# Where the partial sums of the second layer's first product lie in PSUM

## The chip, the core and the metric

The kernel runs on one core of a Trainium2 chip. The metric is the device time of one execution in microseconds (us). The engines are TensorE (PE, with its weight loads as PEld), VectorE (DVE), ScalarE (ACT), GpSimd (POOL) and SyncE (SP), whose queue issues the DMA transfers. Each engine works through its own list of instructions in order, and waits at an instruction until what it needs has been signalled. PSUM, where TensorE leaves its sums, has eight banks here, each of 128 x 512 fp32 values.

## The reference

Attention over chunks of 32 tokens with a local window and 8 memory keys, then two feed-forward layers one behind the other on its 3072 x 512 result:

```python
x = attention(q, k, v, mem_k, mem_v)        # 4 x 8 heads x 768 tokens x 64
h = x @ moe_w_in                            # 3072 x 512 by 512 x 2048
x = (h * sigmoid(1.702 * h)) @ moe_w_out    # 2048 x 512
h = x @ moe2_w_in
return (maximum(h, 0) + alpha * minimum(h, 0)) @ moe2_w_out
```

Weights come as 64-bit floats; the kernel rebuilds fp32 from their words, and splits each fp32 operand into a high and a low fp32r part. A product of two operands is then three matmuls: high by high, high by low, low by high.

## The kernel before

The program has three stages. First come attention and, woven into it, the first layer, in six blocks of 512 tokens: `mm1` (line 425), `act1`, `split_g` and `mm2_t` (line 481), with the second layer's weights prepared beside it. `finish1` (lines 486 to 493) takes the four accumulators of a block, in the PSUM pairs `ya` and `yb`, to `o` tiles by DVE (halves 0 and 2) and ACT (1 and 3), and stores them.

The second layer runs in three rounds (`for P in range(NPAIR)`, line 859) of 1024 tokens each. Its products are done by Strassen's scheme: seven products of half-size blocks in place of eight, in the Winograd form, named p1 to p7 and worked in the order p1, p5, p6, p3, p7, p2, p4 (`PRODUCTS`, line 495). A round has two parts:

- `first` (lines 606 to 644), called for eight blocks (`fp` 0 to 7): for each of the seven products six matmuls of 128x128 by 128x512 (line 619), 42 in a block. Products p1, p6, p7 and p4 add up in one chain, x; p5 and p3 in another, y; p2 stands alone in z. In between the chains are read: behind p1, p5 and p6 ACT copies the state of the chain to SBUF (`snap`, line 603: s1, s5, u2), and behind p3, p7 and p2 DVE adds a copy to it (line 636); p4 is read by the two activation steps of `act2_ops` (lines 452 and 454). So x is read between p1 and p6, between p6 and p7, and between p7 and p4; y between p5 and p3.
- `second` (lines 699 to 751): seven products of 48 matmuls (line 717), four steps of 12 each, from operands that ACT and DVE make just ahead (the ring, lines 657 to 675), with both halves m = 0 and 1 of a tile in use.

PSUM tiles come from pools. `pair(tag, name)` (line 270) gives a tile of two banks; the tags `a`, `ya` and `yb` have one place each, that is six banks, and the tag `h` has two places of one bank each. A new tile of a tag waits until the last readers of the place are done; inside a tile the framework orders a write behind the reads of that tile that stand before it in the program. `two_banks` (line 589) hands out `a`, `ya`, `yb` in rotation: one pair for each block of `first`, whose halves are x and y, and one pair each for x, y and z in `second`.

All instructions of the second layer carry `kp` (line 439), which keeps them in the written order on each engine. `background` (line 458) puts waiting DVE and ACT work (the rest of the activation, the ring) behind the products by a written clock that counts 0.2275 us for a matmul; it is not moved by what really happens. Weight tiles of the second layer stream through ten places, issued by SP ten ahead of their use (`s_ahead`, lines 567 to 585); a block of `first` uses three tiles of 512 KB and one of 256 KB. The last step of the first layer, `do_mm2(len(steps) - 1)`, is called from inside the first block of the layer, behind p5 (lines 643 and 864).

Of the kernel before, what the change touches and what calls it, by code (L numbers as in the profile page):

```python
# [9 lines left out]
F32 = mybir.dt.float32  # L10
# [25 lines left out]
TBM = 512  # L36
# [22 lines left out]
def fused_kernel(ctx: ExitStack, tc: tile.TileContext, qs, ks, vs, ident, w_in1, w_out1, w_in2, w_out2, alpha, out):  # L59
# [10 lines left out]
    ps2 = ctx.enter_context(tc.tile_pool(name="ps2", bufs=2, space=PSUM))  # L70
# [199 lines left out]
    def pair(tag, name):  # L270
        return ps1.tile([128, 2, DM], F32, tag=tag, name=name)
# [147 lines left out]
    def mm1(p, x, n, f):  # L419
        h = ps2.tile([128, TBM], F32, tag="h", name=f"h{p}")  # L420
        wh, wl = wt[p, f]
        i = 0
        for k in range(NKC):
            for w, z in ((wh, 0), (wh, 1), (wl, 0)):
                nc.tensor.matmul(  # L425
                    h[:, :n], w[:, 0, k * 128:(k + 1) * 128], x[:, z, k, :n], start=(i == 0), stop=(i == 3 * NKC - 1)
                )
                i += 1
        return h
# [15 lines left out]
    def vec(cost, fn, after=0.0):  # L445
        clock["v"] = max(clock["v"], after) + cost
        fn()

    def act2_ops(out, c, f, cost):
        t = gp.tile([128, TBM], F32, tag="t", name="t")  # L450
        return [
            (cost, lambda: kp(nc.vector.tensor_scalar(
                out=t, in0=c, scalar1=0.0, scalar2=al_sb[:, f:f + 1], op0=ALU.min, op1=ALU.mult))),
            (0.67, lambda: kp(nc.vector.scalar_tensor_tensor(
                out=out, in0=c, scalar=0.0, in1=t, op0=ALU.max, op1=ALU.add))),
        ]

    def background(until, slot):

        while True:  # L460
            q = later if later else rings if rings and rings[0][2] <= slot else fills if fills and fills[0][2] <= slot else None
            if q is None or clock["v"] + q[0][0] > until:
                return
            cost, fn = q.pop(0)[:2]
            vec(cost, fn)
# [117 lines left out]
    def s_done(n):  # L583
        streamed[1] += n
        s_ahead(streamed[1] + 10)

    npair = [0]

    def two_banks():
        t = pair(("a", "ya", "yb")[npair[0] % 3], f"acc{npair[0]}")  # L590
        npair[0] += 1
        return t

    graw = {}

# [5 lines left out]
    def snap(src, tag, name):  # L601
        t = gp.tile([128, TBM], F32, tag=tag, name=name, bufs=2)
        kp(nc.scalar.copy(t, src))  # L603
        return t

    def first(P, fp, after1=None):
        t = two_banks()
        acc = {"x": t[:, 0], "y": t[:, 1]}
        kept = {}
        for d, n in enumerate(PRODUCTS):  # L610
            if n == "p2":
                acc["z"] = ps2.tile([128, TBM], F32, tag="h", name="hz")
            to = acc[{"p1": "x", "p6": "x", "p7": "x", "p4": "x", "p5": "y", "p3": "y", "p2": "z"}[n]]
            w = units[P, "a", fp, d // 2][:, d % 2]
            hi, lo = xops[P][n]
            i = 0
            for k in range(2):
                for c, x in ((0, hi), (0, lo), (1, hi)):
                    kp(nc.tensor.matmul(  # L619
                        to, w[:, c, k * 128:(k + 1) * 128], x[:, k], start=(i == 0 and n not in ADDED), stop=(i == 5),  # L620
                        skip_group_check=n in ADDED,
                    ))
                    i += 1
            clock["pe"] += 6 * T_MM
            background(clock["pe"], NPROD * fp + d)
            if n == "p1":
                kept["s1"] = snap(to, "gh", "s1")
            elif n == "p5":
                kept["s5"] = snap(to, "gl", "s5")
            elif n == "p6":  # L630
                kept["u2"] = snap(to, "gh", "u2")
            else:
                with_, f, th = {"p3": ("u2", fp, 1), "p7": ("s5", fp + NFP, 1), "p2": ("s1", fp, 0), "p4": (None, fp + NFP, 0)}[n]
                out = graw[f // 2, th][:, f % 2]
                if with_ is not None:
                    vec(0.69, lambda: kp(nc.vector.tensor_tensor(out=out, in0=to, in1=kept[with_], op=ALU.add)), clock["pe"])  # L636
                    later.extend(act2_ops(out, out, f, 0.45))
                else:
                    for cost, fn in act2_ops(out, to, f, 0.75):
                        vec(cost, fn, clock["pe"])  # L640
            if d % 2 == 1 or d == 6:
                s_done(1)
            if n == "p5" and after1 is not None:
                after1()
# [54 lines left out]
    def second(P):  # L699
        acc = {}  # L700
        kept = {}
        last = P == NPAIR - 1
        for q, (d, jj) in enumerate(order):
            n = PRODUCTS[d]
            while (P, d, jj) not in made:
                cost, fn = (later or rings).pop(0)[:2]
                vec(cost, fn)
            key = {"p1": "x", "p6": "x", "p7": "x", "p4": "x", "p5": "y", "p3": "y", "p2": "z"}[n]
            if key not in acc:
                acc[key] = two_banks()  # L710
            to = acc[key]
            hi, lo = ring.pop((P, d, jj))
            w = units[P, "b", d, jj]
            tail = n == "p4" and jj == 3
            for ft, m in [(a, b) for b in range(2) for a in range(2)] if tail else [(a, b) for a in range(2) for b in range(2)]:
                for i, (c, g) in enumerate(((0, hi), (0, lo), (1, hi))):
                    kp(nc.tensor.matmul(  # L717
                        to[:, m], w[:, ft, c, m * 128:(m + 1) * 128], g[:, ft],
                        start=(jj == 0 and ft == 0 and i == 0 and n not in ADDED), stop=(jj == 3 and ft == 1 and i == 2),
                        skip_group_check=n in ADDED,  # L720
                    ))
            clock["pe"] += 12 * T_MM
            background(clock["pe"], NPROD * NFP + q)
            s_done(1)
            while stores:
                kp(nc.sync.dma_start(out=stores[0][0], in_=stores.pop(0)[1]))
            if jj < 3:
                continue
            if n in ("p1", "p5", "p6"):
                tag = {"p1": "gh", "p5": "gl", "p6": "t"}[n]  # L730
                kept[n] = [snap(to[:, m], tag, "k") for m in range(2)]
                continue
            with_, mh, th = {"p3": ("p6", 0, 1), "p7": ("p5", 1, 1), "p2": ("p1", 0, 0), "p4": (None, 1, 0)}[n]
            for m in range(2):
                o = op.tile([128, TBM], F32, tag="o", name="o2")
                r = 256 * mh + 128 * m
                cols = out[r:r + 128, P * PAIR + th * TBM:P * PAIR + (th + 1) * TBM]
                if with_ is not None:
                    vec(0.69, lambda: kp(nc.vector.tensor_tensor(out=o, in0=to[:, m], in1=kept[with_][m], op=ALU.add)), clock["pe"])
                elif m == 0 or not last:  # L740
                    vec(0.69, lambda: kp(nc.vector.tensor_copy(o, to[:, m])), clock["pe"])
                else:
                    c = TBM // 2
                    kp(nc.vector.tensor_copy(o[:, :c], to[:, m, :c]))
                    kp(nc.scalar.copy(o[:, c:], to[:, m, c:]))
                    kp(nc.sync.dma_start(out=cols[:, :c], in_=o[:, :c]))
                    kp(nc.sync.dma_start(out=cols[:, c:], in_=o[:, c:]))
                    continue
                stores.append((cols, o))
                if last and tail:  # L750
                    kp(nc.sync.dma_start(out=stores[0][0], in_=stores.pop(0)[1]))
# [19 lines left out]
    t = ps2.tile([128, 128], F32, tag="h", name="warm")  # L771
# [54 lines left out]
    for i, (p, j, t0, n, f) in enumerate(steps):  # L826
# [8 lines left out]
        h = mm1(p, xt[j], n, f)  # L835
# [23 lines left out]
    for P in range(NPAIR):  # L859
        g_alloc(P)  # L860
        clock["pe"] = clock["v"] = 0.0
        ring_plan(P)
        for fp in range(NFP):
            first(P, fp, (lambda: do_mm2(len(steps) - 1)) if P == 0 and fp == 0 else None)
        if P + 1 < NPAIR:
            x_load(P + 1)
            fills.extend((1.2, fn, NPROD * NFP + XSLOT) for fn in x_steps(P + 1))
        second(P)
        npair[0] += 1
        while fills:  # L870
            fills.pop(0)[1]()

# [40 lines left out]
```

## Time and profile before

| | |
|---|---|
| median of 3 runs | 1197.61 us (1195.74 to 1198.02) |
| the profiled execution, its own time | 1196.13 us |
| its span | 1194.3 us |
| PE, DVE, ACT busy | 1098.5, 766.5, 409.8 us (92%, 64%, 34%) |
| share of the chain that ended last | PE 84%, DVE 7%, ACT 5%, DMA 2%, issue 2% |
| granted TensorE clock | full from about 60 us to the end |

The span runs from the first to the last instruction; the time of the execution is a little longer. The page's strip of 40 slices shows PE at nine tenths or more from the 7th slice on, apart from three stretches at seven to eight tenths: those are the three calls of `first`. In the rows below a matmul's length of 0.39 us is its way through the engine; the next one starts some 0.23 us after it, so what a matmul costs is read from start to start.

### The profile page before, as it was taken

Reading aid. Unit: us, or ns where it says so; the run is one execution under the profiler, and the core shown is the slowest. Engines: PE = TensorE matmul, PEld = TensorE weight load, DVE = VectorE, ACT = ScalarE, POOL = GpSimd, SP = SyncE. Lnnn points to the kernel's source line nnn. Section 1 sums busy time; section 2 is a strip of 40 time slices with the busy share of each in tenths; the row PEclk is TensorE's granted clock in tenths of the full one; section 3 lists DMA queues with packets and bytes.
Section 4 is the critical chain, followed back from the end, with each engine's and each line's share of the span. In section 5 each row is a group of like instructions: output and inputs, shape, how many; then the busy total and the mean of one; then the engine's idle time right before and its main releaser. Section 6 shows DMA issues by size and latency. Waiting matters only on the chain.

```text
span 1194.3 us, 18378 instructions
## 1 busy us (share of the span) xinstructions
PE 1098.5 (92%) x7516; PEld 860.7 (72%) x7516; DVE 766.5 (64%) x1090; ACT 409.8 (34%) x633; POOL 0.2 (0%) x4
## 2 busy tenths in 40 slices
PE   5799999999999999999998878998778999877998
PEld 4677788888878878887886556886555886555786
DVE  5899645676767667766223555975455986554865
ACT  3566423344344335334221111452111452111342
POOL 0000000000000000000000000000000000000000
PEclk6799999999999999999999999999999999999999
DMA  8654332556555466444304445775444866444661
GB/s 299 232 188 154 100 100 89 187 184 213 191 203 206 145 209 234 164 149 162 104 1 123 138 144 174 247 217 166 139 131 142 286 209 184 129 149 146 197 198 71
DMA packets 84098, 200.23 MB, mean 168 GB/s; under 512 B 9520, under 2 KB 26288, under 8 KB 84016
## 3 DMA queue, kind: packets, MB, share of 16 engines
q1 hardware_dynamic: 84016, 199.07, 51.1%
q8 instruction: 59, 0.97, 0.3%
q14 instruction: 23, 0.19, 0.0%
HBM read 157.10 MB, written 41.94 MB: 167 GB/s over the span
## 4 chain that ended last, share of the span: by engine, by line
PE 84%; DVE 7%; ACT 5%; DMA 2%; issue 2%; SPq 0%; DVEq 0%; ACTq 0%
PE h L425 20%; PE acc L717 19%; PE acc L619 19%; PE ya L481 10%; PE yb L481 10%; PE hz L619 3%; ACT s L603 2%; PE xp L373 2%; DMA wraw<-w_out 2%; DVE g L636 1%; ACT u L603 1%; PE sc L295 1%; DVE wtmp L124 1%; DVE wtmp L127 1%; PE pt L358 1%
## 5 line engine op out<-in xcount | busy, mean ns | idle before, releaser
L425 PE MATMUL h<-x,whi 128*128 128x512 f32 x768 | 246.0, 396 | 3.3 <-ACT whi L137 1.9
L619 PE MATMUL acc<-xh,u 128*128 128x512 f32 x384 | 142.9, 413 | 48.0 <-ACT s L603 31.7
L425 PEld LDWEIGHTS h<-x,whi 128*128 128x128 f32 x768 | 143.6, 189 | 35.4 <-ACT whi L137 2.6
L425 PE MATMUL h<-x,wlo 128*128 128x512 f32 x384 | 152.0, 396 | 0.0
L434 DVE SCALAR_TENSOR_TENSOR t<-t,h 128x512 f32<-128x512 f32 x96 | 65.8, 685 | 124.6 <-ACT t L433 124.2
L619 PEld LDWEIGHTS acc<-xh,u 128*128 128x128 f32 x384 | 71.9, 187 | 91.6 <-ACT s L603 51.9
L717 PE MATMUL acc<-r,u 128*128 128x512 f32 x504 | 121.1, 395 | 0.0
L717 PE MATMUL acc<-rx,u 128*128 128x512 f32 x504 | 118.5, 390 | 0.0
L433 ACT ACTIVATE t<-h 128x512 f32<-128x512 f32 x96 | 57.5, 599 | 163.5 <-PE h L425 163.3
L717 PEld LDWEIGHTS acc<-r,u 128*128 128x128 f32 x504 | 94.5, 187 | 22.8
L717 PEld LDWEIGHTS acc<-rx,u 128*128 128x128 f32 x504 | 94.4, 188 | 21.0 <-DVE rx L672 0.5
L603 ACT COPY s<-acc 128x512 f32<-128x512 f32 x48 | 28.1, 585 | 235.7 <-PE acc L619 235.7
L619 PE MATMUL acc<-xw,u 128*128 128x512 f32 x240 | 88.4, 401 | 20.5 <-DVE g L636 20.5
L636 DVE TENSOR_TENSOR g<-acc,u 128x512 f32<-128x512 f32 x24 | 16.6, 692 | 122.8 <-PE acc L619 122.8
L425 PEld LDWEIGHTS h<-x,wlo 128*128 128x128 f32 x384 | 72.4, 189 | 15.6 <-DVE wlo L142 0.3
L471 DVE TENSOR_TENSOR gl<-t,gh 128x512 fp32r<-128x512 f32 x96 | 65.7, 686 | 22.3 <-ACT gh L470 21.1
L481 PE MATMUL ya<-gh,whi 128*128 128x512 f32 x192 | 76.2, 397 | 0.3 <-ACT gh L470 0.3
L481 PE MATMUL ya<-gl,whi 128*128 128x512 f32 x192 | 76.3, 398 | 0.0
L481 PE MATMUL yb<-gl,whi 128*128 128x512 f32 x192 | 75.3, 392 | 0.0
L470 ACT CAST gh<-t 128x512 fp32r<-128x512 f32 x96 | 59.7, 622 | 45.6 <-DVE t L434 41.0
L481 PE MATMUL yb<-gh,wlo 128*128 128x512 f32 x192 | 75.3, 392 | 0.0
L481 PE MATMUL yb<-gh,whi 128*128 128x512 f32 x192 | 75.1, 391 | 0.0
(109 smaller groups left out, 1646.6 us busy)
## 6 DMA issues: line engine op xcount, KB each, us to landing
u<-wo SPq DMA_DIRECT2D x84, 512.0 KB, 4.7
u<-wi SPq DMA_DIRECT2D x72, 512.0 KB, 3.8
v<-vs SPq DMA_DIRECT2D x24, 512.0 KB, 4.2
k<-ks SPq DMA_DIRECT2D x24, 416.0 KB, 4.8
wraw<-w_in SPq DMA_DIRECT2D x16, 512.0 KB, 5.2
wraw<-w_out SPq DMA_DIRECT2D x16, 512.0 KB, 5.7
raw<-w_in SPq DMA_DIRECT2D x32, 256.0 KB, 3.9
wi<-ob SPq DMA_DIRECT2D x16, 512.0 KB, 4.2
```

The source lines that it names most:

```text
L124: nc.vector.scalar_tensor_tensor(out=a, in0=top, scalar=0xC0000000, in1=a, op0=ALU.bitwise_and, op1=ALU.bitwise_or)
L373: nc.tensor.matmul(x[half[z], g, j, c * CHUNK:(c + 1) * CHUNK], s["v"][half[g], c, 2 * j + z, :], s["p"][half[g], 2 * z + j // 2, b * CHUN ...
L425: nc.tensor.matmul(h[:, :n], w[:, 0, k * 128:(k + 1) * 128], x[:, z, k, :n], start=(i == 0), stop=(i == 3 * NKC - 1))
L433: mark["s"] = nc.scalar.activation(out=t[:, :n], in_=h[:, :n], func=AF.Tanh, scale=1.702 / 2).ins
L434: mark["v"] = nc.vector.scalar_tensor_tensor(out=t[:, :n], in0=t[:, :n], scalar=1.0, in1=h[:, :n], op0=ALU.add, op1=ALU.mult).ins
L470: mark["s"] = nc.scalar.copy(gh[:, :n], g[:, :n]).ins
L471: mark["v"] = lo_eng.tensor_tensor(out=gl[:, :n], in0=g[:, :n], in1=gh[:, :n].bitcast(F32), op=ALU.subtract).ins
L481: nc.tensor.matmul(y[m][:, :n], w[:, 1, m * 128:(m + 1) * 128], g[:, :n], start=(f == 0 and i == 0), stop=(f == NF - 1 and i == 2),)
L603: kp(nc.scalar.copy(t, src))
L619: kp(nc.tensor.matmul(to, w[:, c, k * 128:(k + 1) * 128], x[:, k], start=(i == 0 and n not in ADDED), stop=(i == 5), skip_group_check=n in ...
L636: vec(0.69, lambda: kp(nc.vector.tensor_tensor(out=out, in0=to, in1=kept[with_], op=ALU.add)), clock["pe"])
L717: kp(nc.tensor.matmul(to[:, m], w[:, ft, c, m * 128:(m + 1) * 128], g[:, ft], start=(jj == 0 and ft == 0 and i == 0 and n not in ADDED), s ...
```

## The change

Each chain of `first` gets a tile of its own. x takes the first bank of a pair, by turns `a` and `ya` (`x_banks`); y takes the first bank of `yb` in every block; z stays in `h`. In the very first block, when `ya` and `yb` still hold the last accumulators of the first layer, x lies in `a` and y in a tile of the tag `h` (`hy`). In `second`, x takes the next turn of `a` and `ya`, z the other of the two, and y `yb`. The line that moved the rotation on by one after a round is gone. No arithmetic changes.

```diff
--- before.py
+++ after.py
@@ -584,12 +584,13 @@
         streamed[1] += n
         s_ahead(streamed[1] + 10)
 
-    npair = [0]
-
-    def two_banks():
-        t = pair(("a", "ya", "yb")[npair[0] % 3], f"acc{npair[0]}")
-        npair[0] += 1
-        return t
+    turn = [0]
+
+    def x_banks(other=False):
+
+        if not other:
+            turn[0] += 1
+        return pair(("ya", "a")[turn[0] % 2 if not other else 1 - turn[0] % 2], "accx")
 
     graw = {}
 
@@ -604,8 +605,9 @@
         return t
 
     def first(P, fp, after1=None):
-        t = two_banks()
-        acc = {"x": t[:, 0], "y": t[:, 1]}
+        early = P == 0 and fp == 0
+        acc = {"x": x_banks()[:, 0]}
+        acc["y"] = ps2.tile([128, TBM], F32, tag="h", name="hy") if early else pair("yb", "accy")[:, 0]
         kept = {}
         for d, n in enumerate(PRODUCTS):
             if n == "p2":
@@ -707,7 +709,7 @@
                 vec(cost, fn)
             key = {"p1": "x", "p6": "x", "p7": "x", "p4": "x", "p5": "y", "p3": "y", "p2": "z"}[n]
             if key not in acc:
-                acc[key] = two_banks()
+                acc[key] = pair("yb", "accy") if key == "y" else x_banks(key == "z")
             to = acc[key]
             hi, lo = ring.pop((P, d, jj))
             w = units[P, "b", d, jj]
@@ -866,7 +868,6 @@
             x_load(P + 1)
             fills.extend((1.2, fn, NPROD * NFP + XSLOT) for fn in x_steps(P + 1))
         second(P)
-        npair[0] += 1
         while fills:
             fills.pop(0)[1]()
```

What the change does to the lists of the engines is seen at three places. On PE, in the second block of the first round, the first eleven rows are p1, p5 and the start of p6; before, one tile takes all three (`u` is the weight tile, `xh`, `xw`, `xlo0p` are operands):

```order
L619 MATMUL acc_6307<-xh_5867,u_5992 128x512 [waits DMAHW6_49]
L619 MATMUL acc_6307<-xw_1_5869,u_5992 128x512
L619 MATMUL acc_6307<-xh_5867,u_5992 128x512 x2
L619 MATMUL acc_6307<-xw_1_5869,u_5992 128x512
L619 MATMUL acc_6307<-xh_5867,u_5992 128x512
L619 MATMUL acc_6307<-xh_5867,u_5992 128x512 [waits Activation_49]
L619 MATMUL acc_6307<-xlo0p_5872,u_5992 128x512
L619 MATMUL acc_6307<-xh_5867,u_5992 128x512 x2
L619 MATMUL acc_6307<-xlo0p_5872,u_5992 128x512
L619 MATMUL acc_6307<-xh_5867,u_5992 128x512
L619 MATMUL acc_6307<-xh_5867,u_6026 128x512 [waits DMAHW7_49,Activation_49]
```

And now, with `accx` and `accy` as the two tiles:

```order
L621 MATMUL accx<-xh_5867,u_5992 128x512 [waits DMAHW6_49]
L621 MATMUL accx<-xw_1_5869,u_5992 128x512
L621 MATMUL accx<-xh_5867,u_5992 128x512 x2
L621 MATMUL accx<-xw_1_5869,u_5992 128x512
L621 MATMUL accx<-xh_5867,u_5992 128x512
L621 MATMUL accy<-xh_5867,u_5992 128x512
L621 MATMUL accy<-xlo0p_5872,u_5992 128x512
L621 MATMUL accy<-xh_5867,u_5992 128x512 x2
L621 MATMUL accy<-xlo0p_5872,u_5992 128x512
L621 MATMUL accy<-xh_5867,u_5992 128x512
L621 MATMUL accx<-xh_5867,u_6026 128x512 [waits DMAHW7_49,Activation_49]
```

The order is the same; the wait for ACT at the sixth row, the first matmul of p5, is gone, and that at the start of p6 stays. A little further in the same block stand p3 and the first matmul of p7, before:

```order
L619 MATMUL acc_6307<-xh_5867,u_6026 128x512 [waits Activation_49]
L619 MATMUL acc_6307<-xlo0p_5912,u_6026 128x512
L619 MATMUL acc_6307<-xh_5867,u_6026 128x512 x2
L619 MATMUL acc_6307<-xlo0p_5912,u_6026 128x512
L619 MATMUL acc_6307<-xh_5867,u_6026 128x512
L619 MATMUL acc_6307<-xw_0_5868,u_6060 128x512 [waits DMAHW0_49,DVE_49]
```

And now:

```order
L621 MATMUL accy<-xh_5867,u_6026 128x512 [waits Activation_49]
L621 MATMUL accy<-xlo0p_5912,u_6026 128x512
L621 MATMUL accy<-xh_5867,u_6026 128x512 x2
L621 MATMUL accy<-xlo0p_5912,u_6026 128x512
L621 MATMUL accy<-xh_5867,u_6026 128x512
L621 MATMUL accx<-xw_0_5868,u_6060 128x512 [waits DMAHW0_49,Activation_49]
```

At p7 the wait for DVE has become one for ACT. The other blocks show the same. The third place is ACT's list at the first block of the layer (s and u are the copies s1, s5 and u2; `o` is an output of the first layer), before:

```order
L603 COPY s_6222<-acc_6215 128x512 [waits PE_49,Activation_49]
L490 ACTIVATE o<-ya 128x512 [waits DMAHW7_49,DVE_49]
L603 COPY s_6230<-acc_6215 128x512 [waits PE_49]
L490 ACTIVATE o<-yb 128x512 [waits DMAHW6_49,DMAHW4_49,DVE_49]
L603 COPY u_6262<-acc_6215 128x512 [waits PE_49,Activation_49]
```

And now:

```order
L604 COPY s_6223<-accx 128x512 [waits PE_49,Activation_49]
L604 COPY s_6231<-hy 128x512 [waits PE_49]
L490 ACTIVATE o<-ya 128x512 [waits DMAHW7_49,DVE_49]
L490 ACTIVATE o<-yb 128x512 [waits DMAHW6_49,DMAHW5_49,DVE_49]
L604 COPY u_6263<-accx 128x512 [waits PE_49,Activation_49]
```

The copy of y has moved ahead of the two outputs of the first layer, since on PE the six matmuls of p5 now stand ahead of the first layer's last twelve, not behind them. DVE's list is the same in both. On SP one weight tile's load has moved ahead of three stores of the first layer. Apart from these the order of all engines is the same.

## Rows read from the trace of the kernel before

**Rows 1.** Idle time of TensorE before its matmuls, whole span: total us, times, longest.

```profile
PE acc L619 <- ACT s L603: 31.7, 47, 0.7
PE acc L619 <- DVE g L636: 20.5, 24, 0.9
PE acc L619 <- ACT u L603: 16.2, 24, 0.7
```

**Rows 2.** Stretches: length; busy us (x) of PE, PEld, DVE, ACT, POOL; PEclk; DMA; GB/s.

```profile
602.91:608.35 5.44, 5.44 (x26) 4.51 (x24) 1.38 (x2) 1.22 (x2) 0.00 (x0) 1.00 0.00 0
629.02:739.59 110.57, 88.16 (x349) 62.92 (x348) 54.14 (x88) 17.98 (x29) 0.00 (x0) 1.00 0.46 138
739.59:817.17 77.58, 77.58 (x338) 62.95 (x336) 67.62 (x64) 35.86 (x38) 0.00 (x0) 1.00 0.73 234
817.17:925.86 108.69, 85.66 (x337) 60.59 (x336) 53.89 (x87) 16.88 (x27) 0.00 (x0) 1.00 0.46 138
1003.43:1112.13 108.70, 85.67 (x338) 60.57 (x336) 53.90 (x87) 16.89 (x27) 0.00 (x0) 1.00 0.46 138
```

**Rows 3.** Timeline of one block, all engines: start us, us, instruction [idle before <-releaser].

```profile
645.63 0.39 PE L619 MATMUL acc<-xh,u 128*128 128x512 f32 x1
...
646.05 0.58 ACT L603 COPY s<-acc 128x512 f32<-128x512 f32 x1 [8.33 <-PE acc L619]
...
646.69 0.50 PE L619 MATMUL acc<-xh,u 128*128 128x512 f32 x1 [0.68 <-ACT s L603]
...
647.03 0.39 PE L619 MATMUL acc<-xlo0p,u 128*128 128x512 f32 x1
...
647.20 0.69 DVE L454 SCALAR_TENSOR_TENSOR g<-g,t 128x512 f32<-128x512 f32 x1
...
652.62 0.40 PE L619 MATMUL acc<-xh,u 128*128 128x512 f32 x1
...
653.13 0.69 DVE L636 TENSOR_TENSOR g<-acc,u 128x512 f32<-128x512 f32 x1 [5.23 <-PE acc L619]
...
653.85 0.49 DVE L452 TENSOR_SCALAR t<-g,al_sb 128x512 f32<-128x512 f32 x1
...
653.87 0.51 PE L619 MATMUL acc<-xw,u 128*128 128x512 f32 x1 [0.85 <-DVE g L636]
...
654.22 0.40 PE L619 MATMUL acc<-xlo0p,u 128*128 128x512 f32 x1
...
655.57 0.69 DVE L636 TENSOR_TENSOR g<-acc,s 128x512 f32<-128x512 f32 x1 [1.22 <-PE acc L619]
```

**Rows 4.** Timeline of ACT in a block with a cast of a ring.

```profile
661.98 0.58 ACT L603 COPY s<-acc 128x512 f32<-128x512 f32 x1 [1.75 <-PE acc L619]
662.47 1.05 ACT L668 CAST r<-g 128x1024 fp32r<-128x1024 f32 x1
```

**Rows 5.** Timeline of PE: the first 24 matmuls of the second product.

```profile
739.59 5.77 PE L717 MATMUL acc<-r,u 128*128 128x512 f32 x24
```

**Rows 6.** Timeline of ACT at the first block of the layer.

```profile
632.94 0.60 ACT L490 ACTIVATE o<-ya 128x512 f32<-128x512 f32 x1 [1.71 <-DVE o L492]
...
635.23 0.60 ACT L490 ACTIVATE o<-yb 128x512 f32<-128x512 f32 x1
```

**Rows 7.** Timeline of the DMA queue of SP at the first block.

```profile
632.94 1.49 SPq L493 DMA_DIRECT2D y<-o  x3
```

**Rows 8.** Timeline of DVE behind the end of the first round.

```profile
817.37 1.29 DVE L741 COPY o<-acc 128x512 f32<-128x512 f32 x2 [0.90 <-PE acc L717]
```

**Rows 9.** A stretch at the start, columns as in Rows 2.

```profile
12.00:20.00 8.00, 4.78 (x178) 4.11 (x181) 7.83 (x13) 2.56 (x4) 0.00 (x0) 0.50 0.81 309
```

**Rows 10.** Timeline of PE at the start.

```profile
12.30 1.17 PE L295 MATMUL sc<-k,q 64*32 64x64 f32 x64 [6.62 <-DMA k<-ks]
...
41.30 1.20 PE L425 MATMUL h<-x,whi 128*128 128x512 f32 x2
```

**Rows 11.** Line 425: duration ns min/median/max, first and last start.

```profile
L425 PE MATMUL h<-x,whi x768: 387/389/775, 41.3 to 625.7; 128*128 128x512 f32 x192
```

## The prediction

> **What bounds the kernel now.** I read the idle time of TensorE first: the whole span holds three large entries in front of a matmul, all in the second layer's first product, 68.4 us together, and in each TensorE waits for an engine that has just read a partial sum [rows 1]. Then a table of stretches. The three calls of `first` last 110.57, 108.69 and 108.70 us, 327.96 together, with PE busy for 79%; the second product between them and a stretch of the first layer are busy throughout [rows 2]. The two calls that hold nothing else make 13.59 us a block (108.69 / 8). With nothing to wait for, the 24 matmuls of a step of the first layer take 5.44 us, 0.2267 each [rows 2], so that the 42 of a block could take 9.52: some 4.07 us of each block are lost.
>
> The timeline of one block shows where [rows 3]. The last matmul of p1 starts at 645.63, ACT copies x from 646.05 on, and the first matmul of p5, which writes y and has no business with x, starts only at 646.69, 0.04 behind the end of the copy; the one after it starts at 647.03. Two matmul steps thus took 1.40 us in place of 0.453: 0.947 lost. The same stands in front of p6 and p3. In front of p7 the reader is DVE, which adds up p3's y while p7 wants x: 652.62 to 654.22, 1.60 less 0.453, 1.147 lost. Three times 0.947 and 1.147 make 3.99, nearly all of the 4.07. The idle rows count less, since they subtract the modelled tails of the matmuls before. All four waits have one form: a write into one bank is held up by a read of the other bank of the same tile.
>
> **What the change removes.** With x, y and z in separate tiles, each write waits for the reads of its own chain alone. p5 waits for nothing; p6 for s1, p3 for s5, p7 for u2, p4 for DVE's sum over p7, as before. Between a chain's last matmul and its next one stand six matmuls of another chain, so there are seven matmul steps, 1.60 us at 0.228, to cover a read. Do they?
>
> - A copy starts 0.42 behind the start of the last matmul (645.63 to 646.05) and lets the next matmul go 0.64 later (646.69) [rows 3]: 1.06. Margin 0.54.
> - In three blocks of a round a cast of the ring, 1.05 us, stands on ACT between s5 and u2. It starts 0.49 behind s5 [rows 4], and waits for DVE's last activation step, whose end (647.20 + 0.69) lies 2.26 behind p1's last matmul [rows 3], where the earliest cast would lie at 1.37 + 0.42 + 0.49 = 2.28. So it ends near 3.35, u2 was due at 3.16, and is some 0.2 late. Margin 0.33.
> - DVE's list: behind the sum over p3 comes one step of 0.49, done 1.72 behind p3's last matmul (654.34 less 652.62) [rows 3]; the sum over p7 is due at 1.37 + 0.42 = 1.79. p4 can start 0.74 behind the start of that sum (653.13 to 653.87), 1.16 behind p7's last matmul. Margin 0.44, the tightest that repeats in every block. DVE's idle time of 1.22 before this sum shrinks to about 0.07.
> - DVE sits idle for 5.23 before the sum over p3 [rows 3]; 2.84 of it goes with three waits, and 2.39 holds the one ring step (1.22) that two blocks of a round have there. DVE is busy for 54 of 108.7 us now [rows 2]; in 76.6 us that is 70%.
>
> So I expect no new wait in a block. What is late next is TensorE itself.
>
> **What it adds and moves.** y has one place, `yb`, in every block: its next write, p5, comes two products, over 2.7 us, behind the last read's release, so nothing waits. x by turns keeps p1 of a block from waiting for the activation of p4 in the block before, as the rotation did. At the change of rounds the second block wants `a`, whose last copies end at 818.66 [rows 8]; with blocks of 9.58 it starts at 817.17 + 9.58 = 826.75. `second` has three separate tiles before and after: nothing.
>
> In the first block of the layer p5 now stands ahead of the last twelve matmuls of the first layer, which therefore end 1.37 later. On ACT the two outputs of the first layer stand ahead of u2, and the second of them needs the `o` tile that the first store frees. That store was issued at 632.94 [rows 7] and the output started at 635.23 [rows 6], so it takes up to 2.3 us. Now: store at about 634.3, output up to 636.6 to 637.2, u2 behind it in place of 636.1, p7 at 637.85 in place of 637.3. I put 0.5 us for it, once, between 0 and 0.6.
>
> **The rate without waits** is the one term that the trace does not show for p6, p3 and p7, which never ran unhindered. Bounds: 0.2267 in the first layer [rows 2], and 0.2339 for the slower kind of step of the second product ((5.77 - 0.39) / 23 [rows 5]; the whole part is at 77.58 / 336 = 0.2309 [rows 2]). The operands of the first product are those of neither, but its blocks already run p2 and p4 without a wait, and 13.59 less four waits (3.99) is 9.60, that is 0.2286 for 42. I take 0.228. A rule of the Trainium skill, in "TensorE: Matmul & The Clock Gate", section "Wait — 56ns, not 53.3ns?", has back-to-back matmuls of 512 columns at the full clock 215.7 ns apart; by it the sum would be 220.0 us and the time about 1090. The row has 226.7 ns at a granted clock of 1.00, and the measurement decides.
>
> **The sum.** 336 x 3 matmuls and the twelve of the first layer make 1020. At 0.228 they take 232.6, with the 0.5 233.1, where 327.96 stood: 94.9 us less. The bounds are 231.2 (96.7 less) and 238.6 + 0.6 (88.8 less). The profiled execution took 1196.13, which is 1.5 below the median of the runs: 1196.13 - 94.9 = 1101.2, and 1102.7 against the median. I forecast 1102.
>
> **Rivals.**
>
> *DVE takes the place of the wait.* The margin at p4 is 0.44 us, and DVE's own list leaves 0.07 of slack before the sum. If a step slips in front of it, p4 waits like p7 did: 1.147 x 24 = 27.5 less gain, 1130. For it: DVE is the engine that gets denser. Against: its list is unchanged and all its steps have the durations of the rows. Chance 4%.
>
> *The change does half of what it says.* The order shows a wait for ACT at p6 and p3 but not for which copy. If p6 waited for s5 and p3 for u2, two waits of 0.947 stayed in each block: 45.5 less gain, 1148. Against: each would then have to wait for a tile that it does not touch. 3%.
>
> *The weights' supply becomes the bound.* A block needs 3 x 512 + 256 KB, 1.835 MB; in 9.58 us that is 192 GB/s, where 138 flow now. If 138 were the most, a block would take 13.3 us, and 7 us would be gained: 1191. Against: the second product draws 234 GB/s from the same queue without a wait [rows 2], and tiles are asked for ten ahead. 4%.
>
> *The clock falls.* At the start PE waited 6.62 us for a DMA [rows 10], and in the stretch behind it the granted clock was 0.50 [rows 9], the level of 1.2 GHz; the first two matmuls of line 425 then start 0.425 apart (1.20 [rows 10] less the longest single one, 0.775 [rows 11]). If weight tiles came in bursts with pauses of that kind, every matmul at that level would cost 0.197 more: from 482 of the 1020 on (95 / 0.197) the kernel is slower than before, and with all of them at 0.425 it takes 433.5 in place of 328, 1303. Against: now, with four pauses in each block, the granted clock of the first product is 1.00 throughout [rows 2], the level of 2.4 GHz, and pauses go away. 2%. The same page of the Trainium skill, section "A second HAM failure mode: psum-queue depth-cycling", warns that going round PSUM banks lets the engine pause between groups, and the clock swing between its levels; that speaks against a change that puts x in two places by turns. This trace does not bear it out: the kernel goes round three pairs already, at 1.00.
>
> **How the numbers follow.** My forecast has 86%, the four rivals 13%, and 1% is for what I don't see. The forecast's own range goes from 1099 (96.7 less, from the lowest of the runs, 1195.74) to 1109 (88.8 less, from the median); I widen it to 1096 for a rate a little under the row's, and to 1112 for a wait of 0.15 us that stays in each block. This leaves out the rivals. What a measurement can tell from no change is about 0.2%, 2.4 us. Only the clock's fall ends slower, the supply ends faster by 0.5%, or in the worst case with no change: faster 0.96, same 0.02, slower 0.02.
>
> **What would show it.** In the profile after: the three idle entries of TensorE gone or under 5 us together; calls of `first` at about 77 us (the one with the twelve matmuls at 80) and PE busy throughout in them; copies s1, s5 and u2 running while PE goes on; no wait in front of p4; some 190 GB/s in these stretches; the second product still at 77.6. An entry of PE behind DVE's sum with 24 occurrences speaks for the first rival, one behind ACT's copies with 48 for the second, one behind a DMA for the third. I am wrong if a block takes more than 10 us.

## The result, and the profile after

The changed kernel takes 1100.3 us in the median of 4 runs (1098.71 to 1102.19), where the kernel before took 1196.69 beside it: 0.9194 of it, with an interval of 0.9176 to 0.9213. The profiled span is 1098.6 us, 95.7 below the 1194.3 of before. PE's busy share rises from 92% to 97%, DVE's from 64% to 70% with the same busy time (766.3 us).

The table of stretches, with the columns of [rows 2], has the three calls of `first` in its first, third and fourth line, and the second product of one round in its second:

```profile
629.53:709.03 79.50, 79.30 (x349) 65.24 (x348) 54.15 (x88) 17.83 (x29) 0.00 (x0) 1.00 0.64 192
709.03:786.59 77.56, 77.56 (x338) 62.96 (x336) 67.61 (x64) 35.87 (x38) 0.00 (x0) 1.00 0.74 235
786.59:862.75 76.16, 76.16 (x338) 63.08 (x336) 53.91 (x87) 16.75 (x27) 0.00 (x0) 1.00 0.65 196
...
940.30:1016.46 76.16, 76.16 (x337) 63.06 (x336) 53.90 (x87) 16.75 (x27) 0.00 (x0) 1.00 0.67 196
```

The calls of `first` last 79.50, 76.16 and 76.16 us in place of 110.57, 108.69 and 108.70 [rows 2]: 231.82 against 327.96, 96.1 less. The second product stands as it was, 77.56. So the whole gain lies in the stretches that the change touches. Data flow at 192 to 196 GB/s there, and the granted clock is 1.00.

Of TensorE's idle time in the second layer this is left, weight loads (PEld) included (total, times, longest):

```profile
PEld accx L621 <- ACT u L604: 0.6, 1, 0.6
...
PEld accx L719 <- DVE rx L674: 0.5, 3, 0.2
...
PE accx L621 <- ACT u L604: 0.2, 1, 0.2
```

The 68.4 us in three entries [rows 1] have become one wait of 0.2 us at one place. One block after the change, from the timeline of all engines; it answers to [rows 3]:

```profile
643.53 0.39 PE L621 MATMUL accx<-xh,u 128*128 128x512 f32 x1
...
643.75 0.39 PE L621 MATMUL accy<-xh,u 128*128 128x512 f32 x1
...
643.95 0.59 ACT L604 COPY s<-accx 128x512 f32<-128x512 f32 x1 [5.87 <-PE accx L621]
...
644.89 0.19 PEld L621 LDWEIGHTS accx<-xh,u 128*128 128x128 f32 x1
...
645.12 0.39 PE L621 MATMUL accx<-xh,u 128*128 128x512 f32 x1
...
648.97 0.39 PE L621 MATMUL accx<-xw,u 128*128 128x512 f32 x1
...
649.39 0.69 DVE L638 TENSOR_TENSOR g<-accx,s 128x512 f32<-128x512 f32 x1
...
650.55 0.39 PE L621 MATMUL accx<-xw,u 128*128 128x512 f32 x1
```

The last matmul of p1 starts at 643.53, p5's first at 643.75, 0.22 later, while ACT's copy of x starts at 643.95 and runs beside it. The first matmul of p6, on x again, starts at 645.12, 1.59 behind p1's last: seven steps, with no bracket, so it waited for nothing. The same holds for p7's sum (649.39) and p4 (650.55, seven steps behind 648.97).

### The profile page after: what moved, and what is told of

Same layout as the page of the kernel before. It is cut to its first block, busy times and chain, and to the rows that moved or that the text cites. A ratio compares the mean times of both kernels' runs of the same rounds, so it can differ in the third digit from the quotient of the medians.

```text
span 1098.6 us, 18378 instructions
## 1 busy us (share of the span) xinstructions
PE 1070.5 (97%) x7516; PEld 867.9 (79%) x7516; DVE 766.3 (70%) x1090; ACT 409.7 (37%) x633; POOL 0.2 (0%) x4
## 4 chain that ended last, share of the span: by engine, by line
PE 87%; DVE 6%; DMA 3%; ACT 2%; issue 1%; SPq 0%; DVEq 0%; ACTq 0%
PE h L425 21%; PE accx L719 15%; PE accx L621 12%; PE ya L481 11%; PE yb L481 10%; PE accy L719 6%; PE accy L621 6%; PE hz L621 3%; PE xp L373 2%; DMA wraw<-w_out 2%; PE sc L295 1%; DVE wtmp L127 1%; DVE wtmp L124 1%; PE pt L358 1%; DMA y<-o 1%
## 5 line engine op out<-in xcount | busy, mean ns | idle before, releaser
L719 PE MATMUL accx<-r,u 128*128 128x512 f32 x360 | 86.5, 395 | 0.0
L621 PE MATMUL accx<-xw,u 128*128 128x512 f32 x240 | 85.7, 390 | 0.2 <-ACT u L604 0.2
L719 PE MATMUL accx<-rx,u 128*128 128x512 f32 x360 | 84.6, 390 | 0.0
L719 PEld LDWEIGHTS accx<-r,u 128*128 128x128 f32 x360 | 67.5, 187 | 16.3
L719 PEld LDWEIGHTS accx<-rx,u 128*128 128x128 f32 x360 | 67.3, 188 | 15.0 <-DVE rx L674 0.5
L481 PE MATMUL ya<-gh,wlo 128*128 128x512 f32 x192 | 75.1, 391 | 0.0
L604 ACT COPY s<-accx 128x512 f32<-128x512 f32 x24 | 14.1, 589 | 148.4 <-PE accx L621 148.4
L670 ACT CAST rx<-g 128x1024 fp32r<-128x1024 f32 x42 | 44.4, 1057 | 64.7 <-DVE g L454 24.3
L621 PE MATMUL accx<-xh,u 128*128 128x512 f32 x192 | 66.9, 389 | 0.0
```

The source lines that it names most:

```text
L481: nc.tensor.matmul(y[m][:, :n], w[:, 1, m * 128:(m + 1) * 128], g[:, :n], start=(f == 0 and i == 0), stop=(f == NF - 1 and i == 2),)
L621: kp(nc.tensor.matmul(to, w[:, c, k * 128:(k + 1) * 128], x[:, k], start=(i == 0 and n not in ADDED), stop=(i == 5), skip_group_check=n in ...
L670: kp(nc.scalar.copy(ring[P, d, jj][0], src))
L719: kp(nc.tensor.matmul(to[:, m], w[:, ft, c, m * 128:(m + 1) * 128], g[:, ft], start=(jj == 0 and ft == 0 and i == 0 and n not in ADDED), s ...
```

## The experiments

Each kernel is the changed one with the edit shown. Apart from ratios to the kernel before, runs are compared by the length of a block, read from the trace as the distance between the starts of p2's first matmul in blocks that follow each other: 9.52 us in the changed kernel, in every block of a round within 0.03, where 13.60 is what the kernel with shared tiles gives (the first experiment).

**Own tiles undone.** x and y share a tile again, and the turns stay.

```diff
-        early = P == 0 and fp == 0
-        acc = {"x": x_banks()[:, 0]}
-        acc["y"] = ps2.tile([128, TBM], F32, tag="h", name="hy") if early else pair("yb", "accy")[:, 0]
+        both = x_banks()
+        acc = {"x": both[:, 0], "y": both[:, 1]}
```

> The changed kernel with one part undone: in the first product x and y are again the two halves of one tile, which takes a and ya by turns; y's own tile is gone, all else stays. Theory (the loss was four waits a block in which a write of one chain stands behind a read of the other chain in the same tile): all four come back, a block takes 13.6 us, the kernel 1196 us, 96 more than the changed one. Rival (the gain comes from the places, x in two of them by turns and yb free, or from p5 standing ahead of the first layer's last matmuls): the turns stay, so it keeps about 1100 us, or at most the 2 us of the first block are lost.

Measured: 1197.71 us, 0.9999 of the kernel before (0.9988 to 1.0009), a block 13.60 us. TensorE's idle time by releaser:

```profile
PE accx L620 <- ACT s L604: 31.7, 47, 0.7
...
PE accx L620 <- DVE g L637: 20.5, 24, 0.9
...
PE accx L620 <- ACT u L604: 16.3, 24, 0.7
```

These are [rows 1] to a tenth of a microsecond, with the same counts. Shared tiles alone bring the whole loss back, though x still lies in two places by turns and `yb` is free. The rival that put the gain down to the places has fallen.

**The turns undone.** x lies in `a` in every block.

```diff
-        if not other:
-            turn[0] += 1
-        return pair(("ya", "a")[turn[0] % 2 if not other else 1 - turn[0] % 2], "accx")
+        return pair("ya" if other else "a", "accx")
```

> The changed kernel with the other part undone: x lies in a in every block, without turns; x and y keep tiles of their own. Theory (own tiles give the gain, the turns only keep p1 from waiting for the activation of p4 in the block before): p1 waits for the second of DVE's two steps on p4, 1.94 us behind p4's last matmul in place of 0.23, 1.82 with the slower restart, at 24 places, and 1.64 twice at the change of rounds: 47 us more, 1147 us, and no other wait. Rival (one place is enough, since DVE reads p4 at once): 1100 us. Second rival (both parts are needed for any gain): 1196 us.

Measured: 1150.37 us, 0.9604 (0.9587 to 0.962), a block 11.41 us. Idle time of TensorE by releaser, and then the timeline at the start of a block:

```profile
PE accx L619 <- DVE g L454: 33.0, 21, 1.6
...
PE accx L717 <- DVE g L454: 4.7, 3, 1.6
...
PE accx L619 <- DVE o L741: 2.8, 2, 1.4
```

```profile
644.72 0.39 PE L619 MATMUL accx<-xw,u 128*128 128x512 f32 x1
645.14 0.75 DVE L452 TENSOR_SCALAR t<-accx,al_sb 128x512 f32<-128x512 f32 x1 [0.28 <-PE accx L619]
645.93 0.69 DVE L454 SCALAR_TENSOR_TENSOR g<-accx,t 128x512 f32<-128x512 f32 x1
...
646.67 0.50 PE L619 MATMUL accx<-xh,u 128*128 128x512 f32 x1 [1.57 <-DVE g L454]
```

The last matmul of p4 starts at 644.72, DVE's two steps on it follow, and p1's first matmul starts at 646.67, 1.95 behind p4's last; it should have been 0.23. The waits are 26, at the 24 and 2 places expected, and of a block 1.89 us are lost. So own tiles without the turns bring about half of the gain, and the second half hangs on the two places of x. Neither part is enough alone: turns without own tiles bring nothing.

**Twice the copies, into one tile.** ACT makes s1, s5 and u2 twice.

```diff
-        kp(nc.scalar.copy(t, src))
+        for _ in range(2 if name != "k" else 1):
+            kp(nc.scalar.copy(t, src))
```

> The changed kernel in which ACT makes each copy of a partial sum in the first product twice, into the same place, so that the read of the chain ends 0.49 us later. Theory (a read has 0.53 us of room until the chain is written again): no wait in an ordinary block; only in the three blocks of a round with a cast of the ring between s5 and u2 does p7 wait, by some 0.65 us: 6 us in all, 1106 us. Rival (the room is used up, as a read that starts late also delays the next): 0.5 us at each of 72 copies, 35 us, 1135 us. Rival (ACT does not bound these writes at all): 1100 us.

Measured: 1117.22 us, 0.9331 (0.9317 to 0.9345), 17 more than the changed kernel and not 6: a miss. A block takes 10.0 us, with a cast of the ring 10.46. The timeline at p6:

```profile
655.07 0.39 PE L622 MATMUL accx<-xh,u 128*128 128x512 f32 x1
...
655.49 1.21 ACT L605 COPY s<-accx 128x512 f32<-128x512 f32 x2 [5.83 <-PE accx L622]
...
656.75 0.19 PEld L622 LDWEIGHTS accx<-xh,u 128*128 128x128 f32 x1 [0.36 <-ACT s L605]
```

The two copies take 1.21 us, so the second starts some 0.62 behind the first (1.21 less 0.585), not 0.49: two copies of one partial sum into one tile overlap less than two into different tiles (0.48 apart, two experiments below). That is a fault of the edit. But there is a second thing. p6 starts at 656.75, 1.68 behind p1's last (655.07), only 0.09 late, and TensorE's matmul rows have no idle entry there; the weight load of that matmul (PEld) has one, and the next matmul starts 0.34 later (657.09), 0.11 more than a step.

**Four copies into one tile.** As above with `range(4 ...)`.

> As with two copies, but each copy is made four times, so that a read ends 1.47 us later. Theory (room of 0.53 us, then each further delay is a wait of TensorE): p6 waits about 0.9 us, p3 and p7 about 0.5 each, 2.6 us a block with the restarts, 63 us in all, 1163 us; waits for ACT only, none of p5. Rival (ACT does not bound these writes): 1100 us. Rival (each delay counts in full): 1.47 x 72 = 106 us, 1206 us.

Measured: 1190.83 us, 0.9946 (0.993 to 0.9962), a block 12.96, with a cast 13.9. Idle time of TensorE by releaser:

```profile
PE accx L622 <- ACT s L605: 27.0, 23, 1.2
...
PE accx L622 <- ACT u L605: 25.9, 24, 1.7
...
PE accy L622 <- ACT s L605: 15.7, 23, 0.7
```

All waits are for ACT, as the theory has it, and none is p5's (23 for s on y are p3's). The size is a miss, 90 us more and not 63. With 0.62 for each further copy in place of 0.49 a read ends 1.86 later, and the same reckoning that gave 63, with the longer time of ACT for each group of copies, gives about 91; for two copies it gives 14, where 17 were measured. The rival that counts each delay in full would now have 1.86 x 72 = 134.

**One more read, into a tile of its own.** This takes the fault out of the edit.

```diff
+        junk = op.tile([128, TBM], F32, tag="o", name="junk")
...
+            if n in ("p1", "p5", "p6"):
+                kp(nc.scalar.copy(junk, to))
```

> The changed kernel with one more read of each chain: ahead of each copy s1, s5 and u2 ACT copies the same partial sum into a tile that nobody reads. With two copies into one tile the second started 0.62 us behind the first, which was over the room of 0.53; into two tiles copies stand 0.49 apart in the trace. Theory (the room is 0.53 us, sharp): no wait in an ordinary block, and p7 waits in the three blocks of a round with a cast by some 0.65 us: 6 us more than the changed kernel, 1106 us, 10 less than with both copies into one tile. Rival (each further read costs on the whole, whatever the room): 15 us more, 1115 us.

Measured: 1113.85 us, 0.9299 (0.9286 to 0.9313), 11.7 more than the changed kernel beside it (1102.19, 0.9205). Neither 6 nor 15. A block takes about 9.83 us (9.76 to 9.87, and one 10.13), with a cast 10.23. The timeline at p6:

```profile
645.59 0.59 ACT L630 COPY junk<-accx 128x512 f32<-128x512 f32 x1 [5.90 <-PE accx L622]
...
646.07 0.59 ACT L604 COPY s<-accx 128x512 f32<-128x512 f32 x1
...
646.47 0.39 PE L622 MATMUL accy<-xh,u 128*128 128x512 f32 x1
...
646.71 0.19 PEld L622 LDWEIGHTS accx<-xh,u 128*128 128x128 f32 x1 [0.28 <-ACT s L604]
646.72 0.50 PE L622 MATMUL accx<-xh,u 128*128 128x512 f32 x1
...
647.05 0.39 PE L622 MATMUL accx<-xlo0p,u 128*128 128x512 f32 x1
```

The copies do start 0.48 apart. p6's first matmul starts at 646.72, 0.25 behind its predecessor (646.47), hardly late: 0.02. But its weight load starts only at 646.71 with it, where it should have started one step ahead at 646.47, and the matmul behind it comes 0.33 later in place of 0.23. The wait holds up the weight load too. So the room of a read ends at the weight load, one matmul step ahead of the matmul: 0.30 us at p6, not 0.53.

A p3 of the same run shows it without a late matmul:

```profile
657.75 0.39 PE L622 MATMUL accx<-xh,u 128*128 128x512 f32 x1
...
657.91 0.19 PEld L622 LDWEIGHTS accy<-xh,u 128*128 128x128 f32 x1 [0.20 <-ACT s L604]
657.97 0.44 PE L622 MATMUL accy<-xh,u 128*128 128x512 f32 x1
...
658.25 0.40 PE L622 MATMUL accy<-xlo0p,u 128*128 128x512 f32 x1
```

The copy of y, begun at 657.26, lets go at 657.90, 0.15 behind the time of the weight load (657.75, with the matmul before it). The matmul comes 0.22 behind its predecessor, on time, but the one behind it 0.28 later, and 0.05 are lost. Over these runs the loss up to the second matmul is the lateness of the weight load less about 0.11: 0.16 us late cost 0.05, 0.24 late cost 0.13, and 0.65 late, with a cast, cost 0.54 (all in this run); 0.32 late cost 0.21 with two copies into one tile. So the wait begins at the weight load, and time is lost from some 0.11 us behind it.

**A later sum over p7.** One DVE step of 128 x 256, and then of 128 x 512, in front of the sum, to test that at p4, behind DVE's sum. `junk` is a tile as in the experiment before; in the longer step 512 stands for 256.

```diff
+                    if n == "p7":
+                        kp(nc.vector.tensor_tensor(
+                            out=junk[:, :256], in0=kept["s1"][:, :256], in1=kept["s5"][:, :256], op=ALU.add))
```

> The changed kernel with one more DVE step of 128 x 256 (about 0.42 us) in front of the sum over p7 in each block; its result is read by nobody. The sum then starts about 0.30 us late, and p4 may be written at 0.74 behind its start: 0.12 ahead of the time at which p4's first matmul is due, but 0.10 behind the time at which that matmul's weights are loaded. Theory A, from the extra reads on ACT (room counts up to the weight load, one matmul step of 0.227 ahead of the matmul): idle entries of the weight load in front of p4 in all 24 blocks, and about 0.1 us lost in each by the slower restart: 2 to 3 us more than the changed kernel. Theory B (room counts up to the matmul, as in the prediction): no idle, same time. Theory C (the sum is far from deciding): the same as B here and with the longer step.

Measured: 1100.51 us, 0.9189 (0.9175 to 0.9203), against 0.9194 for the changed kernel on the same chip; a block 9.52. Timeline around p4:

```profile
650.96 0.68 DVE L642 TENSOR_TENSOR g<-accx,s 128x512 f32<-128x512 f32 x1
...
651.72 0.19 PEld L622 LDWEIGHTS accx<-xw,u 128*128 128x128 f32 x1
```

The sum starts at 650.96, 0.61 behind p7's last matmul (650.35), only 0.19 late; 0.74 later, at 651.70, p4 may be written, 0.02 ahead of its weight load at 651.72. So the delay stayed just inside both rooms, with no idle entry at p4, and this run tells nothing of which is right.

> As with the shorter step, but 128 x 512 (about 0.69 us): the sum starts about 0.56 late, p4 may be written 0.14 behind the time at which its first matmul is due. Theories A and B: 0.14 and 0.11 for the restart in each of 24 blocks, 6 us more than the changed kernel. Theory C: no difference. A price of 1.147 in each block, the wait that p7 had before, would be 27 us.

Measured: 1103.63 us, 0.9217 (0.9203 to 0.923), 2.6 us more by the medians; a block 9.68, 0.16 more, 3.8 in 24. About half of what was expected, since the sum was late by 0.45 and not 0.56. The timeline around p4:

```profile
647.83 0.39 PE L622 MATMUL accx<-xw,u 128*128 128x512 f32 x1
...
648.70 0.69 DVE L642 TENSOR_TENSOR g<-accx,s 128x512 f32<-128x512 f32 x1
...
649.44 0.19 PEld L622 LDWEIGHTS accx<-xw,u 128*128 128x128 f32 x1 [0.28 <-DVE g L642]
649.44 0.50 PE L622 MATMUL accx<-xw,u 128*128 128x512 f32 x1
...
649.78 0.40 PE L622 MATMUL accx<-xlo0p,u 128*128 128x512 f32 x1
```

p4 was due at 647.83 + 1.587 = 649.42, and may be written from 648.70 + 0.74 = 649.44: 0.02 late as a matmul, and the next one starts at 649.78, 0.34 on: 0.13 lost. The four steps behind that take 0.93 us (to 650.71) in place of 0.907, which makes the 0.16 of the block. The time does not tell the theories apart, as B too was priced with 0.11 for the restart, and the ratios' intervals of this kernel and the changed one overlap. The trace does: the weight load waited for the sum at 23 places (6.5 us in all), and TensorE's own rows have no entry there. With the p3 above, where the matmul was on time and time was lost all the same, B has fallen. Theory C has fallen as well, as the sum does hold p4's weight load.

**y beside z.** y takes the tag `h` in every block.

```diff
-        early = P == 0 and fp == 0
-        acc = {"x": x_banks()[:, 0]}
-        acc["y"] = ps2.tile([128, TBM], F32, tag="h", name="hy") if early else pair("yb", "accy")[:, 0]
+        acc = {"x": x_banks()[:, 0], "y": ps2.tile([128, TBM], F32, tag="h", name="hy")}
```

> The changed kernel with y in the tag h in every block, beside z, so that y and z take its two places by turns and yb stays free in the first product. Theory (what counts is that each chain has a tile of its own, not which bank it lies in): no wait, the same time as the changed kernel, 1100 us, 0.919. Rival (the bank matters, as next to z's it is written while DVE reads z): p5 or p3 waits, some us more, or y waits for z's place: 0.2 to 1 us at 48 places, 1110 to 1150 us.

Measured: 1101.2 us, 0.9196 (0.9184 to 0.9209), as the changed kernel beside it (0.9205). TensorE's waits in the second layer are those of the changed kernel: the weight load's one wait for u2 in the first block (0.6 us) and its three for DVE's `rx` (0.5 us). Of these two places for y neither is better, as long as y is a tile of its own.

**The changed kernel again.** It ran on two more occasions, unaltered, beside the kernels that are compared with it.

> The changed kernel itself, beside the three that follow, so that effects below half a per cent can be read against it: 1100 us, 0.919 of the kernel before.

> The changed kernel itself on the same chip, for the differences of a few microseconds: 0.920 of the kernel before.

Measured: 1102.19 us, 0.9205 (0.9191 to 0.9218), and 1100.99 us, 0.9194 (0.9181 to 0.9208). The ratio comes back within 0.0011 of the first one, so the two later ones serve as the base for the kernels beside them.

**Two places of the ring exchanged in SBUF.** This looks for more, in the second product, where one kind of step is slower.

```diff
-                graw[j, th] = chunk_slot(6 + 2 * (j % 4) + j // 4, th, ...)
+                c = 6 + 2 * (j % 4) + j // 4
+                graw[j, th] = chunk_slot({6: NF - 2, 7: NF - 1}.get(c, c), th, ...)
...
-            return [chunk_slot(NF - 2 + i, z, DIM, F32R, f"{name}{z}") for z in range(2)]
+            return [chunk_slot(6 + i, z, DIM, F32R, f"{name}{z}") for z in range(2)]
```

> The changed kernel with two places of the ring (the moving operands of every second pair of steps in the second product, the slow kind, 24 matmuls in 5.60 us) exchanged in SBUF with two places of the raw activations. Theory (the slow kind is due to where the operand lies in SBUF): these steps come down to the 5.44 to 5.49 us of the others, 504 matmuls by 0.005 to 0.007: 2.5 to 3.4 us less than the changed kernel, 1097 us. Rival (it is due to who writes the operand, or to ACT and DVE at work beside it): the steps stay at 5.60 and the time at 1100 us.

Measured: 1096.24 us, 0.9157 (0.9145 to 0.917), where the changed kernel beside it had 0.9205 (0.9191 to 0.9218): faster than both kernels. First the start of the second product in the changed kernel, then here (PE's timeline):

```profile
709.03 5.77 PE L719 MATMUL accx<-r,u 128*128 128x512 f32 x24
714.64 5.63 PE L719 MATMUL accx<-rx,u 128*128 128x512 f32 x24
```

```profile
709.90 5.60 PE L720 MATMUL accx<-r,u 128*128 128x512 f32 x24
715.35 5.79 PE L720 MATMUL accx<-rx,u 128*128 128x512 f32 x24
...
726.41 5.60 PE L720 MATMUL accy<-rx,u 128*128 128x512 f32 x24
731.85 5.60 PE L720 MATMUL accx<-r,u 128*128 128x512 f32 x24
```

From start to start the changed kernel needs 5.61 us for 24 matmuls with `r`; here they need 5.45 (709.90 to 715.35). The steps with `rx`, whose operand did not move, go from 5.48 to 5.44 (726.41 to 731.85), which the theory did not have; only the first of them is slower here, as its weight loads wait 0.3 us for DVE's `rx`. The second product of the first round goes from 709.90 to 786.25, 76.35 us in place of 77.56, 3.6 for three rounds. The profiled spans of this kernel and the changed one beside it differ by 5.0 (1095.9 and 1100.9); the other 1.4 lie ahead of the first second product, which starts at 709.90 here and at 711.34 there, where the changed kernel's own two traces have 709.03 and 711.34. The engines do the same work and only places in SBUF are exchanged, so the steps do not stay slow because of who writes their operand. But the raw activations that DVE and ACT read and write moved as well, so the run does not show whether the place of the operand alone counts or how these accesses meet.

## Why the prediction was right

**The wait and its cause.** A write into one half of a tile held up by a read of the other half: shown by the undone half (0.9999), with the same three idle entries as before. Four waits a block, 3.99 us by my rows; 13.60 less 9.52 is 4.08. The other 0.09 stand behind the waits: my rows end with the second matmul, and the four steps behind it took 0.93 us (647.03 to 647.96 in the trace of before) in place of 0.907. By its row the copy in front of p5 ends at 646.63, so p5 came 0.06 behind it and not 0.04.

**What covers a read.** I had no new wait in a block, and there is none. The margins, though, were too wide by one matmul step, since I counted them up to the matmul and the wait already holds its weight load. At p6 I put 0.54; the copy at 643.95 lets go at 644.59, the weight load comes at 644.89: 0.30. At p4 I put 0.44; it is 0.19 to 0.21 (649.39 + 0.74 = 650.13, and the load one step ahead of 650.55). In blocks with a cast of the ring I put 0.33; in the trace u2 starts at 656.30 and p7's weight load at 657.13, which leaves 0.19. So the forecast held with less to spare than I thought, and it did not need the difference; but two experiments built on it missed, the first of them in part by the fault of its edit.

**The turns of x.** The prediction gave them a single clause (they keep p1 from waiting for p4's activation, as the rotation did). Undone, they cost some 50 us (1150.37 against 1100.3), half of the gain. The clause was right, and the price was missing.

**The first block.** I put 0.5 us, between 0 and 0.6. After the change, from the timeline of all engines:

```profile
637.01 0.60 ACT L490 ACTIVATE o<-yb 128x512 f32<-128x512 f32 x1 [1.60 <-DMA y<-o]
...
637.51 0.58 ACT L604 COPY u<-accx 128x512 f32<-128x512 f32 x1
637.55 0.39 PE L621 MATMUL hy<-xh,u 128*128 128x512 f32 x1
...
638.14 0.50 PE L621 MATMUL accx<-xw,u 128*128 128x512 f32 x1 [0.20 <-ACT u L604]
...
638.48 0.40 PE L621 MATMUL accx<-xlo0p,u 128*128 128x512 f32 x1
```

The second output of the first layer waits for its `o` tile and starts at 637.01, inside the 636.6 to 637.2 that I had; u2 comes at 637.51 behind it, and p7, due at 637.55 + 0.23 = 637.78, starts at 638.14, the next one 0.34 later: 0.36 and 0.11, 0.47 lost.

**The rate without waits.** I took 0.228 for a matmul and thought it the one open term. The block at 9.52 makes it 0.2267, the first layer's rate and my lower bound: 1020 x 0.2267 = 231.2, with 0.47 231.7, against 231.82 measured. That is the 1.2 us between my 94.9 and the 96.1 of the trace. The 0.2286 that I had derived from 13.59 less the four waits was too high, since it spread the 0.09 us of slow steps behind the waits over the whole block. The 215.7 ns that the Trainium skill's page "TensorE: Matmul & The Clock Gate" gives in its section "Wait — 56ns, not 53.3ns?" were seen nowhere in the second layer's first product; the measurement stands, 226.7 at a granted clock of 1.00.

**The rivals.** DVE did not take the place (no entry behind it), though the 128 x 512 step shows that it can: a sum 0.45 us late cost 0.16 a block, not 1.147. The change did what it says. The supply rose from 138 to 196 GB/s without a wait for a DMA, and the granted clock stayed at 1.00, its level of 2.4 GHz, with x in two places by turns. The warning of the same page of the Trainium skill, section "A second HAM failure mode: psum-queue depth-cycling", is not borne out here: neither kernel shows a clock below 1.00 in these stretches.

## What to carry to other kernels

Look for an engine that waits for the reader of a neighbour: two chains in two banks of one tile are one thing to the framework, and cost here 4 us in each 13.6. Give each chain that is read while another is written a tile of its own, and two places by turns where its next round starts before the last read is done; here the turns alone gave nothing and the own tiles alone half. When you reckon how late a read may end, count up to the weight load in front of the matmul; in these runs a load late by more than 0.11 us cost the rest of its lateness.

## What was not expected of the hardware

A wait at a matmul holds its weight load as well, so that a delay which hardly moves the matmul itself (0.02 us) still cost 0.13 us up to the next matmul and 0.16 in the block. The idle column of PE's own rows does not show it; PEld's does.

The matmuls of the second product ran at 5.61 us for 24 when their moving operand lay in the two last chunks of the weight area, and at 5.45 when it had changed places with raw activations in two chunks in the middle, with the same instructions. What it is in these places that costs 7 ns a matmul stays open, and so does why the steps whose operand did not move gained 0.04 us each.
